# Linear attention, a routed expert layer and a feed-forward layer in one kernel: batchwise attention in four chain groups, filler on the first weights, rows gathered seven tiles ahead

## The chip, the cores and the metric

The kernel runs on one core of a Trainium2 chip. A core has a matrix engine (PE, with its weight loads shown apart as PEld), three engines for elementwise work (DVE, ACT, POOL), a queue processor that issues transfers (SP) and 16 DMA engines. The metric is the device time of one execution in microseconds (us), less is better; several runs are taken and their median counts. A profile is one more execution with its trace.

## The reference, cut to what matters

```python
kv  = einsum('bhsd,bhse->bhde', k, v)           # 4 batches, 8 heads, 576 rows, 64 wide
out = einsum('bhsd,bhde->bhse', q, kv)
x   = out / sqrt(mean(out**2) + 1e-6) * g_norm  # as 2304 rows of 512
logits = x @ w_gate                             # 8 experts
e, gate = argmax(logits), softmax(logits)[argmax]
# rows in order of arrival go to their expert, at most `capacity` (576) each
h = relu(rows_e @ w1[e]); y = h @ w2[e]         # 512 -> 1024 -> 512 per expert
x2[row] = gate * y
h2 = x2 @ w_in; g = where(h2 > 0, h2, exp(h2) - 1)
result = g @ w_out                              # 512 -> 2048 -> 512
```

## The kernel before, in words

All products are in float32; the large ones are done as three products of split operands (a rounded high part and the remainder; `three`, L585). There are 18 tiles of 128 rows.

**Attention** (L57 to L360). SP issues the loads of k and v chunk by chunk (`load_kv`) and of q in pieces (`load_q`), then the stores of the results to `x_dram`, in one queue. The order of everything else is written out by hand between `fill(6)` and the last `step(cc, ...)`. `kv_product(b, n0, n1)` multiplies chunks of a batch, `kv_out`, `kv_turn` and `kv_gate` turn the product into the matrix `kva[b]`, which has eight gate columns per head beside the values, `out_tile(i)` multiplies the rows of tile i by it, and ACT and POOL copy and square the result. `out_sums(i)` adds the squares on DVE. `fill(n)` issues n products of a constant on PE that nothing reads; `fill(n, t)` first waits for the tile t.

**Chains and dispatch** (L223 to L452). `chain(i0, G)` computes the norm, the gate logits and the one-hot choice `oh` of G tiles together, 17 small steps that `step(c, n)` advances, most of them on DVE. The groups hold 4, 5 and 9 tiles. When the last group has its `oh`, two products count the rows per expert (`p_tot`, `p_pos`), a scan (`incl`) and some twenty DVE instructions make the permutation, and `p_inv` gives `ids`, the row numbers in expert order.

**Experts** (L505 to L860). POOL gathers the permuted rows from `x_dram` tile by tile (`gather`, L491) into buffers `xg`, of which there are three; DVE scales a tile (`place_scale`, L497), PE transposes it (`place_turn`, L503) and ACT copies it to `xT`. The gather of tile a+3 stands behind the transposes of tile a, which free its buffer. The experts come in order of their row count, in windows of 352, 336, ... rows. A unit u is one of the 8 chunks of one expert's hidden width: `expert_h(u)` is 12 products into a PSUM tile `ph`, `expert_y(u)` 12 products into `acc`. `step(u)` loads the weights of unit u+3, runs `expert_h(u)`, places a row tile or more, runs `expert_y(u-1)`, places more, and splits the weights of unit u+2 (on ACT, DVE and POOL). `QUOTA` gives how many tiles the units of the first expert place; before unit 6 all 18 have to be placed, 3 in `first_window` and 15 in the units 0 to 5.

**Feed-forward** (L820 to L925). 96 steps in which PE multiplies for 4.2 us each; the loads and splits of these weights are spread over all units.

Of the kernel before, what the change touches and what calls it, by code (L numbers as in the profile page):

```python
# [9 lines left out]
F32 = mybir.dt.float32  # L10
# [31 lines left out]
def block_kernel(ctx, tc, qT, k, v, g_norm, w_gate, w1, w2, w_in, w_out, out, cap, **_):  # L42
# [62 lines left out]
    with ExitStack() as actx:  # L105
# [80 lines left out]
        groups = [(0, 4), (4, 5), (9, 9)]  # L186
        GM = 9
# [35 lines left out]
        def chain(i0, G):  # L223

            def t_(shape, name):
                full = ap2.tile([P, GM] + shape, F32, name=name)
                return full[:, :G]
# [53 lines left out]
        for c in range(9, 18):  # L281
            load_kv(c)
        load_q(2, [(0, 256), (256, S)])
        load_q(3, [(0, 192), (192, 448), (448, S)])
        fill(6)

        ca, cb, cc = (chain(*g) for g in groups)
        for c in range(5):
            kv_product(0, c, c + 1)
            fill(3 if c < 4 else 0)  # L290
        kv_out(0)
        kv_product(1, 0, 1)
        fill(1)
# [5 lines left out]
        kv_product(1, 1, 3)  # L299
        out_tile(1)  # L300
        out_sums(0)
        out_tile(2)
        out_sums(1)
        kv_product(1, 3, 5)
        kv_out(1)
        out_tile(3)
        out_sums(2)
        kv_turn(1)
        fill(3)
        kv_gate(1)  # L310
        out_sums(3)
        fill(1)
        step(ca, 2)
        out_tile(4)
        step(ca, 4)
        kv_product(2, 0, 2)
        out_tile(5)
        out_sums(4)
        step(ca, 4)
        kv_product(2, 2, 4)  # L320
        out_tile(6)
        out_sums(5)
        step(ca, 3)
        kv_product(2, 4, 5)
        kv_out(2)
        kv_product(3, 0, 1)
        fill(2)
        kv_turn(2)
        out_sums(6)
        step(ca, 4)  # L330
        out_tile(7)
        kv_gate(2)
        out_sums(7)
        kv_product(3, 1, 3)
        out_tile(8)
        out_sums(8)
        step(cb, 2)
# [3 lines left out]
        fill(2)  # L341
        kv_turn(3)
        step(cb, 2)
        fill(2)
        kv_gate(3)
        fill(1)
        step(cb, 1)
        for i in range(9, NT):
            out_tile(i)
            if i > 9:  # L350
                out_sums(i - 1)
            step(cb, 2 if i < 14 else 1 if i == 14 else 0)
        out_sums(17)
        fill(6)
        step(cc, 2)
        fill(3, flat(made[9]["a"]))
        step(cc, 2)
        fill(2, flat(made[9]["e"]))
        step(cc, 2)
        fill(2, flat(made[9]["z"])[:, 0:P])  # L360
        step(cc, 2)
        fill(1, flat(made[9]["lg"]))
        step(cc, 4)
# [11 lines left out]
        step(cc, 5)  # L375
# [11 lines left out]
        nc.vector.tensor_tensor(out=pos, in0=incl, in1=p_pos, op=ALU.add)  # L387
        before = t_(EE, "before")
        nc.vector.tensor_tensor(out=before, in0=key[:, None, :].to_broadcast(EE), in1=key.to_broadcast(EE), op=ALU.is_gt)
        off, kept = vals[:, 1], vals[:, 2]  # L390
# [3 lines left out]
        fill(4, flat(bk))  # L394
# [12 lines left out]
        nc.vector.tensor_reduce(out=tab, in_=rr, axis=AX, op=ALU.add)  # L407
        dest = t_([P, NT], "dest")
        nc.vector.tensor_reduce(out=dest, in_=pos.rearrange("p e c -> p c e"), axis=AX, op=ALU.add)
        nc.vector.tensor_copy(tabi, tab[0:1])  # L410
        fill(4, flat(tab))
# [8 lines left out]
        fill(2, flat(oa))  # L420
# [70 lines left out]
    def gather(a):  # L491
# [464 lines left out]
```

## Time and profile before

| | us |
|---|---|
| median of three runs | 724.04 (721.87 to 725.79) |
| the profiled execution | 721.96 |
| its span | 720.2 |
| PE busy in the span | 692.4 (96%) |
| DVE, ACT, POOL busy | 425.3, 347.8, 96.9 |
| mean granted clock of PE | 0.982 |

Times in the trace run from the span's start. The share of PE is an average: in the long stretch of experts and feed-forward it is without a gap, and the gaps are all in the first 126 us. The granted clock is 1.00 at PE's upper level (2.4 GHz) and 0.50 at its lower one (1.2 GHz).

### The profile page before, as it was taken

What the parts mean: (1) busy time and instruction counts of PE and PEld (TensorE: products, weight loads), DVE (VectorE), ACT (ScalarE), POOL (GpSimd) and SP (SyncE); (2) the same over time, 40 slices, a digit from 0 to 9 for tenths busy, and PEclk for the clock granted to TensorE, in tenths of its full rate; (3) what the DMA queues carried; (4) which work ended last, traced back from release to release, by engine and by line L of the source; (5) the groups of instructions that cost most, each with busy time, mean ns of one, the idle gap of its engine ahead of it and who ended that gap; (6) DMA issues with size and microseconds to landing.
All of it is one profiled execution on the core that took longest, in us unless ns stands there. A gap on an engine that the chain in (4) does not pass through costs nothing.

```text
span 720.2 us, 11582 instructions
## 1 busy us (share of the span) xinstructions
PE 692.4 (96%) x4310; PEld 645.6 (90%) x4310; DVE 425.3 (59%) x789; ACT 347.8 (48%) x689; POOL 96.9 (13%) x108
## 2 busy tenths in 40 slices
PE   7997787999999999999999999999999999999996
PEld 6987787999998999999999998998999999899895
DVE  4567655767876878655555545666994334333342
ACT  1552554455555655566566554444654334333331
POOL 7121472000000000052222000000000000011122
PEclk9998798999999999999999999999999999999999
DMA  8995774556555657435335434333542223233312
GB/s 286 397 304 142 218 214 130 176 172 197 170 181 155 218 165 253 133 132 190 146 118 217 163 117 147 118 146 118 196 154 90 103 115 119 101 132 131 132 45 87
DMA packets 55423, 117.53 MB, mean 163 GB/s; under 512 B 8000, under 2 KB 21824, under 8 KB 55360
## 3 DMA queue, kind: packets, MB, share of 16 engines
q1 hardware_dynamic: 51744, 107.12, 43.8%
q0 software_dynamic: 2880, 9.59, 3.9%
q8 instruction: 36, 0.59, 0.3%
q14 instruction: 27, 0.22, 0.1%
q10 hardware_dynamic: 736, 0.02, 0.1%
HBM read 97.68 MB, written 19.02 MB: 162 GB/s over the span
## 4 chain that ended last, share of the span: by engine, by line
PE 59%; issue 8%; POOL 1%; POOLq 0%; DVE 0%
PE ph L587 10%; PE ph L589 10%; PE ph L588 10%; PE acc L887 8%; PE acc L888 8%; PE acc L886 8%; PE acc L589 2%; PE acc L587 2%; PE acc L588 2%; POOL out L897 1%; POOLq L952 0%; DVE part L894 0%; POOLq L897 0%
## 5 line engine op out<-in xcount | busy, mean ns | idle before, releaser
L867 DVE SCALAR_TENSOR_TENSOR g<-e,ph 128x384 f32<-128x384 f32 x96 | 53.0, 552 | 133.6 <-ACT e L865 133.3
L589 PE MATMUL ph<-yl,w1h 128*128 128x384 f32 x384 | 129.5, 337 | 0.0
L587 PE MATMUL ph<-yh,w1h 128*128 128x384 f32 x384 | 129.3, 337 | 0.0
L588 PE MATMUL ph<-yh,w1l 128*128 128x384 f32 x384 | 129.0, 336 | 0.0
L864 ACT ACTIVATE e<-ph 128x384 f32<-128x384 f32 x96 | 47.2, 492 | 160.8 <-PE ph L589 160.7
L888 PE MATMUL acc<-w2h,gl 128*128 128x512 f32 x288 | 114.0, 396 | 0.0
L887 PE MATMUL acc<-w2l,gh 128*128 128x512 f32 x288 | 113.7, 395 | 0.0
L886 PE MATMUL acc<-w2h,gh 128*128 128x512 f32 x288 | 112.0, 389 | 0.0
L587 PE MATMUL ph<-xh,w1h 128*128 128x288 f32 (+6 forms) x256 | 79.2, 309 | 2.4 <-PEq L734 1.7
L589 PE MATMUL ph<-xl,w1h 128*128 128x288 f32 (+6 forms) x256 | 78.5, 306 | 0.0
L588 PE MATMUL ph<-xh,w1l 128*128 128x288 f32 (+6 forms) x256 | 78.4, 306 | 0.0
L587 PE MATMUL acc<-hh,w2h 128*128 128x288 f32 (+6 forms) x256 | 77.5, 303 | 0.0
L588 PE MATMUL acc<-hh,w2l 128*128 128x288 f32 (+6 forms) x256 | 77.0, 301 | 0.0
L589 PE MATMUL acc<-hl,w2h 128*128 128x288 f32 (+6 forms) x256 | 76.9, 301 | 0.0
L587 PEld LDWEIGHTS ph<-yh,w1h 128*128 128x128 f32 x384 | 72.2, 188 | 4.2
L588 PEld LDWEIGHTS ph<-yh,w1l 128*128 128x128 f32 x384 | 72.1, 188 | 4.1
L589 PEld LDWEIGHTS ph<-yl,w1h 128*128 128x128 f32 x384 | 72.0, 188 | 0.0
L480 ACT ACTIVATE gh<-g 128x384 fp32r<-128x384 f32 x96 | 50.4, 525 | 43.1 <-DVE g L867 41.3
L483 DVE TENSOR_TENSOR gl<-g,gh 128x384 fp32r<-128x384 f32 x96 | 55.7, 580 | 18.1 <-ACT gh L480 18.1
L606 ACT ACTIVATE hh<-ph 128x288 fp32r<-128x288 f32 (+6 forms) x64 | 27.1, 423 | 81.0 <-PE ph L589 81.0
L888 PEld LDWEIGHTS acc<-w2h,gl 128*128 128x128 f32 x288 | 54.0, 187 | 11.6
L887 PEld LDWEIGHTS acc<-w2l,gh 128*128 128x128 f32 x288 | 54.0, 187 | 9.2
(157 smaller groups left out, 1188.1 us busy)
## 6 DMA issues: line engine op xcount, KB each, us to landing
a<-w SPq DMA_DIRECT2D x128, 256.0 KB
yh<-y_dram SPq DMA_DIRECT2D x18, 768.0 KB
yl<-y_dram SPq DMA_DIRECT2D x18, 768.0 KB
w<-w_in SPq DMA_DIRECT2D x16, 512.0 KB
w<-w_out SPq DMA_DIRECT2D x16, 512.0 KB
kt<-k SPq DMA_DIRECT2D x18, 256.0 KB
vt<-v SPq DMA_DIRECT2D x18, 256.0 KB
x_dram<-oz_all SPq DMA_DIRECT2D x18, 256.0 KB
```

The source lines that it names most:

```text
L480: return nc.scalar.activation(dst[0], src, AF.Copy)
L483: return engine.tensor_tensor(out=dst[1], in0=src, in1=dst[0].bitcast(F32), op=ALU.subtract)
L587: nc.tensor.matmul(out, lhsT=ah, rhs=bh, start=start, stop=False)
L588: nc.tensor.matmul(out, lhsT=al, rhs=bh, start=False, stop=False)
L589: nc.tensor.matmul(out, lhsT=ah, rhs=bl, start=False, stop=stop)
L606: nc.scalar.activation(hh[:, :W], ph[:, :W], AF.Relu)
L864: nc.scalar.activation(e, ph[:, :BT], AF.Relu, scale=-1.0)
L867: nc.vector.scalar_tensor_tensor(out=g, in0=e, scalar=-1.0, in1=ph[:, :BT], op0=ALU.add, op1=ALU.max)
L886: nc.tensor.matmul(acc, lhsT=gh[:, ts], rhs=w2h, start=(c == 0), stop=False)
L887: nc.tensor.matmul(acc, lhsT=gh[:, ts], rhs=w2l, start=False, stop=False)
L888: nc.tensor.matmul(acc, lhsT=gl[:, ts], rhs=w2h, start=False, stop=(c == NC2 - 1))
L897: put = nc.gpsimd.indirect_dma_start(out=out, out_offset=bass.IndirectOffsetOnAxis(ap=ids[:, i:i + 1], axis=0), in_=part[:, i], in_offset= ...
```

## The change

Five edits that are made together.

1. Attention in another hand-written order: q of batch 2 is loaded before the last four chunks of k and v, out tiles 9 to 12 stand between the steps of batch 3, and most fillers of this part are gone. In the first five chunks a filler now reads the chunk of k that has landed.
2. Four chain groups of 4, 5, 3 and 6 tiles. The addition of 1e-9 to the softmax's sum and the product `rr` move from DVE to POOL, and the conversion `tabi` stands before `dest` on DVE.
3. In the dispatch the fillers behind `oa` are fewer, and one more group waits for `incl`.
4. 16 products of a constant with the first four weight tiles, in the order of their landing, behind the 14 fillers that follow `p_inv`.
5. Four more row buffers (`lent`), lent by the second pair of window buffers, so that seven gathers stand at the front; the gather of tile a+7 stands behind the transposes of tile a. Two PSUM tiles for the transposed rows and two for `ph`, in place of one and three. `QUOTA` is 2 for the units 0 to 5. The weights of unit 2 wait for the third gather, not the second. The staging pool of the weights is allocated first, over the space of k and v.

```diff
-        groups = [(0, 4), (4, 5), (9, 9)]
+        groups = [(0, 4), (4, 5), (9, 3), (12, 6)]
...
-            yield V.tensor_scalar(out=sm, in0=sm, scalar1=1e-9, scalar2=None, op0=ALU.add)
-            yield V.reciprocal(out=sm, in_=sm)
-            V.tensor_tensor(out=rr, in0=r[:, :, None, :].to_broadcast([P, G, 2, H]), in1=sm.to_broadcast([P, G, 2, H]), op=ALU.mult)
+            yield nc.gpsimd.tensor_scalar(out=sm, in0=sm, scalar1=1e-9, scalar2=None, op0=ALU.add)
+            V.reciprocal(out=sm, in_=sm)
+            nc.gpsimd.tensor_tensor(out=rr, in0=r[:, :, None, :].to_broadcast([P, G, 2, H]), in1=sm.to_broadcast([P, G, 2, H]), op=ALU.mult)
...
-        for c in range(9, 18):
+        for c in range(9, 14):
             load_kv(c)
         load_q(2, [(0, 256), (256, S)])
+        for c in range(14, 18):
+            load_kv(c)
         load_q(3, [(0, 192), (192, 448), (448, S)])
...
         kv_out(3)
         step(cb, 1)
-        fill(2)
+        out_tile(10)
         kv_turn(3)
+        out_sums(9)
+        step(cb, 3)
+        out_tile(11)
+        kv_gate(3)
...
-        fill(2, flat(oa))
+        fill(2, flat(tab))
+        fill(0, flat(oa))
...
+    wst = ctx.enter_context(tc.tile_pool(name="wst", bufs=2, reuse_waits="tile"))
     xw = ctx.enter_context(tc.tile_pool(name="xw", bufs=2, reuse_waits="tile"))
     hp = ctx.enter_context(tc.tile_pool(name="hp", bufs=3, reuse_waits="tile"))
-    wst = ctx.enter_context(tc.tile_pool(name="wst", bufs=2, reuse_waits="tile"))
...
-    ps_h = ctx.enter_context(tc.tile_pool(name="ps_h", bufs=3, space=PSUM, reuse_waits="tile"))
-    ps_x = ctx.enter_context(tc.tile_pool(name="ps_x", bufs=1, space=PSUM, reuse_waits="tile"))
+    ps_h = ctx.enter_context(tc.tile_pool(name="ps_h", bufs=2, space=PSUM, reuse_waits="tile"))
+    ps_x = ctx.enter_context(tc.tile_pool(name="ps_x", bufs=2, space=PSUM, reuse_waits="tile"))
...
-    XG = 3
+    XG, XE = 3, 4
...
+    def gather():
+        a = gathered["n"]
+        if a >= NT:
+            return
+        gathered["n"] += 1
+        k = a % (XG + XE)
+        if k >= XG:
+            xg_t[a] = lent[k - XG]
+        else:
+            xg_t[a] = wst.tile([P, C + 2 * H], F32, name="xg", tag="w64", bufs=XG)
...
-    QUOTA = (1, 2, 2, 3, 2, 2, 3, 0)
+    QUOTA = (2, 2, 2, 2, 2, 2, 3, 0)
...
-        gathers = [gather(a) for a in range(XG)]
+        for tag in ("xh", "xl"):
+            t = xw.tile([P, XE // 2, C + 2 * H], F32, name="lent", tag=tag)
+            lent.extend(t[:, n] for n in range(XE // 2))
+        gathers = [gather() for _ in range(XG + XE)]
+
+        idle = ps_h.tile([P, C], F32, name="idle", tag="ph")
+        for t in wstage[0] + wstage[1]:
+            for _ in range(4):
+                nc.tensor.matmul(idle[:, 0:P], lhsT=ident, rhs=t[:, 0:P], start=True, stop=True)
         expert_split(0, nc.vector)
         expert_split(1, nc.vector)
         first_window()
-        tc.add_manual_dep(expert_load(2).ins, gathers[1].ins.name, ...)
+        tc.add_manual_dep(expert_load(2).ins, gathers[2].ins.name, ...)
```

POOL at the beginning of the experts, before: `L494 DMA` rows are gathers, `w1l` is POOL's share of a weight split, one per unit.

```order
L383 COPY vals<-row 128x8
L494 DMA xg<-x_dram,ids 128x528 x7
L483 TENSOR_TENSOR w1l<-a_1022,w1h 128x512
L494 DMA xg<-x_dram,ids 128x528 x2
L483 TENSOR_TENSOR w1l<-a_1028,w1h 128x512
L494 DMA xg<-x_dram,ids 128x528 x2
L483 TENSOR_TENSOR w1l<-a_1066,w1h 128x512
L494 DMA xg<-x_dram,ids 128x528 x3
```

POOL at the same place after the change (L542 gathers, L521 splits):

```order
L419 COPY vals<-row 128x8
L256 TENSOR_TENSOR rr<-r,sm 128x96
L542 DMA xg<-x_dram,ids 128x528 x3
L542 DMA lent<-x_dram,ids 128x528 x4
L542 DMA xg<-x_dram,ids 128x528 x3
L542 DMA lent<-x_dram,ids 128x528 x2
L521 TENSOR_TENSOR w1l<-a_1078,w1h 128x512
L542 DMA lent<-x_dram,ids 128x528 x2
L521 TENSOR_TENSOR w1l<-a_1084,w1h 128x512
L542 DMA xg<-x_dram,ids 128x528 x2
L521 TENSOR_TENSOR w1l<-a_1129,w1h 128x512
```

Seven gathers wait for no row buffer, where three did; 12 of the 18 stand before the first split in place of 7.

PE from `p_inv` to the first products of unit 0, before (`pt` are transposes of rows, four to a tile; `ob` is a weight of `p_inv`):

```order
L437 LDWEIGHTS ob
L437 MATMUL p_inv<-oat,ob 128x18
L120 MATMUL idle<-ident 128x128 x14
L561 MATMUL pt<-ident,xg 128x128 x12
L587 MATMUL ph<-xh,w1h 128x352
L588 MATMUL ph<-xh,w1l 128x352
L589 MATMUL ph<-xl,w1h 128x352
```

PE at the same place after the change:

```order
L475 LDWEIGHTS ob
L475 MATMUL p_inv<-oat,ob 128x18
L120 MATMUL idle<-ident 128x128 x14
L884 MATMUL idle<-a_990,ident 128x128 x4
L884 MATMUL idle<-a_991,ident 128x128 x4
L884 MATMUL idle<-a_994,ident 128x128 x4
L884 MATMUL idle<-a_995,ident 128x128 x4
L609 MATMUL pt<-ident,xg 128x128 x12
L635 MATMUL ph<-xh,w1h 128x352
```

The transposes of the first window stand behind 16 products that wait for the four weight tiles.

DVE from the last `oh` to the scan, before (`sm` is the softmax's sum, `incl` the scan's result):

```order
L250 TENSOR_TENSOR oh<-sel,m_767 128x9x8
L253 TENSOR_REDUCE sm<-ex 128x9
L254 TENSOR_SCALAR sm<-sm 128x9
L255 RECIPROCAL sm<-sm 128x9
L256 TENSOR_TENSOR rr<-r,sm 128x144
L377 SCALAR_TENSOR_TENSOR incl<-reset,p_tot 128x144
```

DVE at the same place after the change:

```order
L250 TENSOR_TENSOR oh<-sel,m_791 128x6x8
L255 RECIPROCAL sm<-sm 128x5
L255 RECIPROCAL sm<-sm 128x3
L253 TENSOR_REDUCE sm<-ex 128x6
L413 SCALAR_TENSOR_TENSOR incl<-reset,p_tot 128x144
```

The last `oh` is of 6 tiles, not 9; three instructions stand between it and the scan where four stood, two of them left over from the groups before, and the last group's own reciprocal has moved behind the scan.

## Rows read from the trace of the kernel before

**Rows 1.** Stretches (us): each engine's busy time (instructions), granted clock, DMA share, GB/s.

```profile
53.75:67.70 13.95, 11.25 (x77) 9.95 (x78) 11.49 (x41) 3.09 (x9) 0.00 (x0) 0.76 0.51 107
67.70:78.10 10.40, 5.83 (x40) 5.20 (x38) 7.50 (x17) 4.43 (x8) 5.02 (x5) 0.76 0.81 247
78.10:126.30 48.20, 41.53 (x240) 39.45 (x241) 25.07 (x34) 25.25 (x44) 24.86 (x23) 0.88 0.60 180
126.30:700.00 573.70, 571.97 (x3308) 535.92 (x3307) 343.25 (x619) 289.29 (x578) 39.31 (x37) 1.00 0.42 149
```

**Rows 2.** The same view, cut where the granted clock changes.

```profile
73.00:83.30 10.30, 7.52 (x29) 6.50 (x29) 5.82 (x9) 4.31 (x8) 2.93 (x3) 0.50 0.80 267
114.00:120.80 6.80, 6.00 (x22) 5.62 (x23) 2.76 (x3) 3.31 (x6) 1.28 (x1) 0.50 0.02 5
```

**Rows 3.** PE's waits from 78 to 126.4: us in total, times, longest.

```profile
PE pt L507 <- DVE xg L500: 4.3, 3, 2.5
```

**Rows 4.** DVE's waits in the same stretch.

```profile
DVE xg L500 <- DMA xg<-x_dram,ids: 13.7, 7, 3.1
```

**Rows 5.** Timeline of PE (start, duration): the first products of five units.

```profile
78.11 0.66 PE L587 MATMUL ph<-xh,w1h 128*128 128x352 f32 x1 [0.67 <-ACT xh L563]
...
88.00 0.40 PE L587 MATMUL ph<-xh,w1h 128*128 128x352 f32 x1
...
92.71 0.40 PE L587 MATMUL ph<-xh,w1h 128*128 128x352 f32 x1
...
122.48 0.32 PE L587 MATMUL ph<-xh,w1h 128*128 128x352 f32 x1
...
126.31 0.32 PE L587 MATMUL ph<-xh,w1h 128*128 128x336 f32 x1
```

**Rows 6.** Timeline of the first and third gather, and of the third tile's scaling.

```profile
68.71 1.17 POOL L494 DMA_INDIRECT xg<-x_dram,ids  x1 [16.79 <-DMA a<-w]
...
71.59 0.95 POOL L494 DMA_INDIRECT xg<-x_dram,ids  x1 [0.30 <-issue]
...
75.45 0.75 DVE L500 SCALAR_TENSOR_TENSOR xg<-xg,used 128x512 f32<-128x512 f32 x1 [0.24 <-DMA xg<-x_dram,ids]
```

**Rows 7.** Stretch of attention, PE's fillers alone: PE and PEld busy, clock, DMA, GB/s.

```profile
17.30:52.00 34.70, 3.80 (x22) 2.92 (x22) 1.00 1.11 355
```

**Rows 8.** Timeline of DVE: the last group's chain and the scan.

```profile
53.79 0.20 DVE L234 TENSOR_SCALAR a<-sums 128x72 f32<-128x72 f32 x1
...
55.42 0.76 DVE L241 TENSOR_TENSOR z<-oz_all,r 128x576 f32<-128x576 f32 x1
56.21 1.19 DVE L244 TENSOR_REDUCE lg<-z 128x72 f32<-128x576 f32 x1
...
58.50 0.47 DVE L250 TENSOR_TENSOR oh<-sel,m 128x72 f16<-128x72 f32 x1
...
59.82 0.46 DVE L377 TENSOR_TENSOR_SCAN incl<-reset,p_tot 128x144 f32<-128x144 f32 x1
```

**Rows 9.** Groups by line and shape: z and lg of five tiles (busy us, mean ns).

```profile
L244 DVE TENSOR_REDUCE lg<-z 128x40 f32<-128x320 f32 x1 | 0.7, 728 | 0.0
...
L241 DVE TENSOR_TENSOR z<-oz_all,r 128x320 f32<-128x320 f32 x1 | 0.5, 492 | 0.0
```

**Rows 10.** Timeline of the end of the dispatch.

```profile
64.06 1.95 DVE L433 TENSOR_TENSOR ob<-neg,nb 128x768 f16<-128x768 f16 x2
...
66.91 0.60 PE L437 MATMUL p_inv<-oat,ob 128*128 128x18 f16 x18
...
67.55 0.18 DVE L445 TENSOR_SCALAR ids<-p_inv 128x18 uint32<-128x18 f32 x1 [1.24 <-PE p_inv L437]
```

**Rows 11.** Timeline of one hand-over of `ph`: last product, DVE's read, next-but-one product.

```profile
292.03 0.28 PE L589 MATMUL ph<-xl,w1h 128*128 128x256 f32 x1
...
292.76 0.42 DVE L607 SCALAR_TENSOR_TENSOR hl<-ph,hh 128x256 fp32r<-128x256 f32 x1
...
296.45 0.28 PE L587 MATMUL ph<-xh,w1h 128*128 128x256 f32 x1
```

More of the change, by code (lines that the diff above doesn't have):

```diff
@@ L225, in t_ @@
             def t_(shape, name):
-                full = ap2.tile([P, GM] + shape, F32, name=name)
+                full = ap2.tile([P, GM] + shape, F32, name=name, bufs=3)
                 return full[:, :G]
@@ L280, in block_kernel, with chunk @@
         load_q(1, [(0, 320), (320, S)])
-        for c in range(9, 18):
+        for c in range(9, 14):
             load_kv(c)
         load_q(2, [(0, 256), (256, S)])
+        for c in range(14, 18):
+            load_kv(c)
         load_q(3, [(0, 192), (192, 448), (448, S)])
+        def chunk(b, n, after):
+            fill(1, kt[(b // 2) * 9 + (b % 2) * 4 + n][:, 0:P])
+            kv_product(b, n, n + 1)
+            fill(after)
+        ca, cb, cc, cd = (chain(*g) for g in groups)
         fill(6)
-        ca, cb, cc = (chain(*g) for g in groups)
         for c in range(5):
-            kv_product(0, c, c + 1)
-            fill(3 if c < 4 else 0)
+            chunk(0, c, (3, 3, 4, 3, 0)[c])
         kv_out(0)
         kv_product(1, 0, 1)
-        fill(1)
         kv_turn(0)
@@ L340, in block_kernel @@
         step(cb, 1)
-        fill(2)
+        out_tile(10)
         kv_turn(3)
-        step(cb, 2)
-        fill(2)
-        kv_gate(3)
-        fill(1)
-        step(cb, 1)
[L348 to L352, printed above, removed]
+        out_sums(9)
+        step(cb, 3)
+        out_tile(11)
+        kv_gate(3)
+        out_sums(10)
+        step(cb, 2)
+        out_tile(12)
+        out_sums(11)
+        step(cb, 3)
+        step(cc, 1)
+        out_tile(13)
+        step(cc, 1)
+        out_sums(12)
+        step(cb, 2)
+        step(cc, 2)
+        out_tile(14)
+        step(cb, 1)
+        out_sums(13)
+        step(cc, 2)
+        out_tile(15)
+        out_sums(14)
+        step(cc, 3)
+        out_tile(16)
+        out_sums(15)
+        step(cc, 1)
+        out_tile(17)
+        step(cc, 2)
+        out_sums(16)
         out_sums(17)
+        L = groups[-1][0]
         fill(6)
[L355 to L363, printed above, removed]
+        step(cd, 1)
+        step(cb, 1)
+        step(cd, 1)
+        step(cc, 1)
+        fill(3, flat(made[L]["a"]))
+        step(cc, 1)
+        step(cd, 2)
+        fill(2, flat(made[L]["e"]))
+        step(cd, 2)
+        fill(2, flat(made[L]["z"])[:, 0:P])
+        step(cb, 1)
+        step(cc, 1)
+        step(cd, 2)
+        fill(1, flat(made[L]["lg"]))
+        step(cd, 4)
+        step(cb, 1)
+        step(cc, 1)
         def t_(shape, name, dt=F32):
@@ L374, in block_kernel @@
         fill(2)
-        step(cc, 5)
+        step(cd, 3)
         incl = t_([P, E, NT], "incl")
@@ L486, in ring_tiles @@
         return [ring.tile([P, C], F32R, name=n) for n in ("w1h", "w1l", "w2h", "w2l")]
-    XG = 3
+    XG, XE = 3, 4
     xg_t = {}
-    def gather(a):
-        if a < NT:
+    lent = []
+    gathered = {"n": 0}
+    def gather():
[7 more added lines that the diff above has]
+        else:
             xg_t[a] = wst.tile([P, C + 2 * H], F32, name="xg", tag="w64", bufs=XG)
-            return nc.gpsimd.indirect_dma_start(out=xg_t[a], out_offset=None, in_=x_dram,
-                                         in_offset=bass.IndirectOffsetOnAxis(ap=ids[:, a:a + 1], axis=0))
+        return nc.gpsimd.indirect_dma_start(out=xg_t[a], out_offset=None, in_=x_dram,
+                                            in_offset=bass.IndirectOffsetOnAxis(ap=ids[:, a:a + 1], axis=0))
     def place_scale(a):
@@ L508, in place_turn @@
         nc.scalar.activation(xT[:, :, a * P:(a + 1) * P], pt, AF.Copy, scale=g_col)
-        gather(a + XG)
+        gather()
     offs, eids = {}, {}
@@ L563, in first_window @@
             nc.scalar.activation(xh[:, :, w], pt[:, :, :w.stop - w.start], AF.Copy, scale=g_col)
-            gather(a + XG)
+            gather()
             pts.append(pt)
```

53 lines of the change are left out of this document (29 added, 24 removed).

## The prediction

> **What bounds the kernel now.** I read the stretches first. From 126.3 us to 700 PE is busy 571.97 of 573.70 us at the upper clock [rows 1]: nothing that the change does ahead of 126.3 can hide there, and what is won or lost before moves the end by as much. The change touches only what lies before, so the question is when the second expert starts (126.31, the last of [rows 5]). Three stretches lead to it. Attention up to 52 us is bound by the loads: 355 GB/s and a DMA share above 1, with PE at the upper clock and 22 filler instructions in it [rows 7]. From 53.75 to 67.7 the chain of the last group and the permutation run on DVE (11.49 of 13.95 us busy). From 67.7 to 78.1 the rows and the first weights arrive and PE is busy for 5.83 of 10.40 us. From 78.1 to 126.3 the first expert runs: the clock is 0.88 in the mean and the DMA share only 0.60 [rows 1].
>
> The waits tell why. In the first expert PE waits 4.3 us for scaled rows [rows 3], and DVE, before it can scale them, 13.7 us in seven waits for gathers [rows 4]. The gather of tile a+3 starts only when tile a is transposed; the first gather starts at 68.71 and the third at 71.59, yet the third tile is scaled at 75.45 [rows 6]: some 4 us from issue to use. With three buffers the row supply is a loop of that latency. The idle time has a second price: the clock stood at 0.50 from 73.0 to 83.3 and from 114.0 to 120.8, each time after PE had idled [rows 2].
>
> **The change part by part.**
>
> *Attention and dispatch, up to `ids` (67.73 in the trace, from [rows 10]: 67.55 + 0.18).* PE loses 14 of its 22 filler instructions here (11 fills become 4); at 2.92/22 = 0.133 us each that is 1.8 us of PE [rows 7]. But DVE now has the chain of three more tiles to do before the last sums, some 2.7 us (z and lg at about 0.16 and 0.23 us less than those of [rows 9] for two tiles fewer, eleven more instructions at 0.2 like the first of [rows 8]), late, since the data arrive late. I give PE 1.8 and take most of it back on DVE: the last sums end 0.5 us earlier (bounds: 1.8 earlier, 0.9 later, when DVE takes all of its 2.7). Then the last chain: with 6 tiles between the rows of 5 and 9, z takes 0.492 + (0.757 - 0.492)/4 = 0.56 in place of 0.76 us and lg 0.84 in place of 1.19, and seven small instructions some 0.02 less each [rows 8, 9]: 0.7 us. Between `oh` (ends at 58.97) and the scan (59.82) three instructions of 0.2 stand for 0.85 us, which wins 0.25; the reciprocal that now comes behind the scan costs 0.2: nothing. POOL's two new instructions per group feed only the store of `rr` and that reciprocal, with some 1 us of DVE work before it; if POOL were late there, DVE would stand still for as long. Last, `p_inv` starts at 66.91 although `ob` is ready at 64.06 + 1.95 = 66.01 [rows 10]: PE was held by fillers at the lower clock. With four fewer of their instructions behind `oa` 0.7 of these 0.9 us go. Sum: `ids` 1.9 us earlier (bounds: 3.4 earlier, 0.9 later).
>
> *From `ids` to the first product of unit 0: 78.11 - 67.73 = 10.38 us.* What ends last is the third tile. POOL's distance from gather to gather stays, so its scaling ends at `ids` + 8.47 (75.45 + 0.75 - 67.73) [rows 6]. From there 1.9 us were transposes and copies at the lower clock. The 16 new products read weights that land before the rows, so at the upper clock (32 instructions of 0.133 us, 4.3 us, from the end of the 14 fillers at about `ids` + 3) they end at about `ids` + 7.3, ahead of the third tile; PE goes into the transposes without the idle time of before: 0.6 us (bounds: 1 us, or a loss of 2, when they run at the lower clock and the transposes stand behind them). The weights no longer wait for the end of `ob`, which takes them off the DMA engines when the rows come; I count that as nothing.
>
> *The first expert: 48.2 us.* When nothing waits, a unit with two tiles takes 92.71 - 88.00 = 4.71 us and one without 126.31 - 122.48 = 3.83 [rows 5]. With seven gathers ahead, tile a+7 is requested three units before its use, some 14 us, against the 4 us of latency. So: unit 0 has no `expert_y` (4.71 - 1.92 = 2.8), units 1 to 4 take 4 x 4.71 = 18.84, unit 5 has three tiles more, at DVE's 0.75 each [rows 6] since two PSUM tiles now let PE run ahead of ACT's copies (4.71 + 2.25 = 6.96), units 6 and 7 take 2 x 3.83 = 7.66. Sum 36.3 us: 11.9 less (bounds: 13 less, when unit 5's tiles cost PE alone; nothing, when the rows come no faster). POOL has two gathers of 1.3 and a split of 1.3 us in a unit of 4.71, so it keeps up. The same bytes, 180 GB/s x 48.2 us = 8.7 MB, in 36.3 us are 239 GB/s; the core moved 247 with the same mixture just before [rows 1] and 267 at its densest [rows 2]. That is close, and is the second rival.
>
> *Two PSUM tiles for `ph`, for all 160 units and steps.* The read-out of a `ph` ends at 292.76 + 0.42 = 293.18, and the next-but-one product starts at 296.45 [rows 11]: 3.3 us to spare where the products are shortest. Cost: nothing.
>
> Sum: 1.9 + 0.6 + 11.9 = 14.4 us off the span of 720.2; with the 1.76 us around it the profiled execution's 721.96 become 707.6. It lies 2.1 below the median of its runs. Part of their scatter of 3.9 us must be where in the clock's changes the waits fall, and most of those waits go; I take half of the 2.1 and forecast 708.5.
>
> **Rivals.** *A cold start.* PE still waits between the last filler and unit 0, with 12 transposes in some 3 us. In the trace such a stretch ended at 1.2 GHz: from 73.0 to 83.3 [rows 2]. Then unit 0's product takes twice its 1.92 us and the transposes 0.3 more, about +2.2, and if it lasts as long as before (10.3 us at half speed) 5 us: 710.7 to 713.5, taken as 711. For it: the wait for the third tile stays. Against: the filler ends some 1 us before that tile, not 3. The Trainium skill's page "TensorE: Matmul & The Clock Gate" (Part 1) says that "the default state is throttled, and activity releases the throttle"; by that rule fillers protect the clock only while they run, and this rival is what it makes of the change. The trace agrees with it, at 0.50 after both idle stretches.
>
> *The transfers set the pace.* If the DMA engines give no more than the middle of 180 and 247 GB/s, 213, the first expert's 8.7 MB take 40.8 us and 7.4 are won there: 713. For it: in this stretch the engines are already 0.60 busy, and gathers and weights share them. Against: DVE waited for a gather that had been issued late, not for one in a queue.
>
> *Only attention and dispatch give something,* and the rows stay as late (a lent buffer comes free too late, say): 2.5 us, 719.5 to 721.5, no change.
>
> *Slower: two `ph` are too few.* If the read-out of `ph` came over 3.3 us later than now, PE would wait in each unit and step. The gain is lost from 0.09 us in each of 160; at 0.2 us, net 18 us later: 726. For it: DVE is the busiest of the engines behind PE, and it reads each `ph`. Against: PE never waited for it in 573.7 us, and the spare time is 3.3 us.
>
> **How the numbers follow.** Forecast 0.57, cold start 0.24, transfers 0.12, no change 0.04, slower 0.03. About 0.5% (3.6 us) is what a measurement can tell from no change: faster takes the first three, 0.93, same 0.04, slower 0.03. The likeliest case has 704.5 (all terms at their good ends but the 0.9 of DVE) to 710.5; the range reaches through the cold start and half of the transfers' case: 704.5 to 713.
>
> **What would show it.** Seven gathers on POOL at distances of 1.3 us right behind `ids`; `ids` at 65.8; unit 0 at about 75.6 with the granted clock at 1.00; units 1 to 4 each 4.7 us apart; PE's wait for scaled rows under 1 us; the second expert at about 111.9 in place of 126.31, and the rest as long as before, 594 us. Wrong it is if DVE's waits for gathers stay near 13.7 us, if the DMA share from unit 0 on is above 0.9 with PE waiting, or if PE waits for DVE's `hl` or `g`.

## The result, and the profile after

The changed kernel takes 711.79 us (median of four runs, 710.62 to 712.05) against 723.35 (721.87 to 725.79) for the kernel before on the same chip: 0.9829 of it, 95% interval 0.9803 to 0.9855. The forecast was 708.5 in a range of 704.5 to 713: faster, as forecast, by 11.6 us in place of some 15. A second series of the changed kernel gave 711.29 (ratio 0.9836, 0.9815 to 0.9857).

The profiled execution took 710.62 us, with a span of 708.7. The page has PE busy for 689.5 us (97%) at a mean granted clock of 0.998. Its stretches, cut at the same four events as [rows 1] (length; busy time and instructions of PE, PEld, DVE, ACT, POOL; granted clock; DMA share; GB/s):

```profile
54.89:66.74 11.85, 9.27 (x73) 7.32 (x74) 10.38 (x42) 3.46 (x11) 1.78 (x7) 1.00 0.57 140
66.74:75.85 9.11, 8.11 (x71) 7.64 (x70) 7.25 (x16) 4.10 (x8) 6.97 (x7) 1.00 0.72 193
75.85:112.90 37.05, 36.32 (x240) 35.09 (x241) 27.66 (x35) 24.91 (x44) 24.33 (x21) 1.00 0.70 232
112.90:688.90 576.00, 572.61 (x3310) 536.37 (x3309) 343.38 (x620) 289.81 (x579) 39.12 (x37) 1.00 0.43 149
```

The first expert has shrunk from 48.20 to 37.05 us, PE is busy for 36.32 of them, and the clock is 1.00 where it was 0.88. The same rows and weights now come at 232 GB/s with the DMA share at 0.70, so the transfers did not set the pace over the whole of it. The last row has a loss: PE is idle for 3.4 us there, against 1.7 in [rows 1].

PE's waits in the first expert (us in total, times, longest), which answer to [rows 3]:

```profile
PE ph L635 <- ACT xh L611: 0.7, 1, 0.7
PE pt L555 <- ACT xT L556: 0.3, 1, 0.3
PE pt L555 <- PE pt L555: 0.3, 1, 0.3
```

No wait for scaled rows is left (4.3 us before). DVE's waits for gathers, the 13.7 us of [rows 4], are now:

```profile
DVE lent L548 <- DMA lent<-x_dram,ids: 3.0, 3, 1.2
```

These 3.0 us are early, while POOL issues gather after gather: the fifth, sixth and seventh gather are issued at 72.67, 74.08 and 75.60 and DVE can scale their rows from 78.28, 80.66 and 82.12, 5.6 to 6.6 us later and not 4. PE feels 0.3 of these waits: the last of its three lines above is the second tile of unit 0, whose row is scaled only at 79.03. The gathers on POOL stand right behind `ids` (66.74), 1.25 to 1.63 us apart (start, duration):

```profile
67.04 1.33 POOL L542 DMA_INDIRECT xg<-x_dram,ids  x1 [5.78 <-DMA a<-w]
68.67 1.18 POOL L542 DMA_INDIRECT xg<-x_dram,ids  x1 [0.30 <-issue]
70.16 0.95 POOL L542 DMA_INDIRECT xg<-x_dram,ids  x1 [0.30 <-issue]
71.41 0.96 POOL L542 DMA_INDIRECT lent<-x_dram,ids  x1 [0.30 <-issue]
```

PE's timeline from `p_inv` to the second expert, cut to the fillers, the transposes of the first three tiles and the first products of the units 0, 1, 2 and of the second expert (112.91, 126.31 in [rows 5]):

```profile
66.38 3.37 PE L120 MATMUL idle<-ident 128*128 128x128 f32 x28
69.58 3.74 PE L884 MATMUL idle<-a,ident 128*128 128x128 f32 x32
73.16 1.04 PE L609 MATMUL pt<-ident,xg 128*128 128x128 f32 x8
74.52 0.66 PE L609 MATMUL pt<-ident,xg 128*128 128x128 f32 x4 [0.33 <-DVE xg L548]
75.85 0.43 PE L635 MATMUL ph<-xh,w1h 128*128 128x352 f32 x1 [0.67 <-ACT xh L611]
...
79.52 0.41 PE L635 MATMUL ph<-xh,w1h 128*128 128x352 f32 x1
...
84.31 0.41 PE L635 MATMUL ph<-xh,w1h 128*128 128x352 f32 x1
...
112.91 0.32 PE L635 MATMUL ph<-xh,w1h 128*128 128x336 f32 x1
```

Up to the second expert 13.4 us are gone. The span is shorter by 11.5 only, so 1.9 came back later, in a stretch of which the forecast said that nothing changes. PE's waits behind the second expert's start show where. Before:

```profile
PE ph L587 <- PEq L734: 1.7, 1, 1.7
```

After:

```profile
PE ph L635 <- ACTq L782: 2.4, 1, 2.4
PE acc L636 <- issue: 1.0, 1, 1.0
```

L734 and L782 are the same statement: the conditional pass over rows beyond the windows (`beyond_windows`), which this input never enters. All engines test a value there and jump over the pass, and PE has nothing to do until its own jump is done.

### The profile page after: what moved, and what is told of

It reads as the page before. It is cut to its first block, busy times and chain, and to the rows that moved or that the text cites. A ratio compares the mean times of both kernels' runs of the same rounds, so it can differ in the third digit from the quotient of the medians.

```text
span 708.7 us, 11682 instructions
## 1 busy us (share of the span) xinstructions
PE 689.5 (97%) x4344; PEld 643.1 (91%) x4344; DVE 428.9 (61%) x796; ACT 347.8 (49%) x692; POOL 100.4 (14%) x116
## 4 chain that ended last, share of the span: by engine, by line
issue 45%; PE 22%; POOL 2%; POOLq 0%; ACT 0%
PE ph L635 4%; PE ph L637 4%; PE ph L636 4%; PE acc L636 2%; PE acc L635 2%; PE acc L637 2%; POOL out L953 2%; PE acc L943 1%; PE acc L944 1%; PE acc L942 1%; POOL yl L521 1%; POOLq L1008 0%; ACT yh L518 0%; ACT e L920 0%; POOLq L953 0%
## 5 line engine op out<-in xcount | busy, mean ns | idle before, releaser
L521 DVE TENSOR_TENSOR gl<-g,gh 128x384 fp32r<-128x384 f32 x96 | 54.9, 571 | 19.0 <-ACT gh L518 19.0
L944 PEld LDWEIGHTS acc<-w2h,gl 128*128 128x128 f32 x288 | 54.0, 188 | 11.6
```

Of the source, the lines that this page charges most:

```text
L521: return engine.tensor_tensor(out=dst[1], in0=src, in1=dst[0].bitcast(F32), op=ALU.subtract)
L944: nc.tensor.matmul(acc, lhsT=gl[:, ts], rhs=w2h, start=False, stop=(c == NC2 - 1))
```

## The experiments

Each kernel was timed against the kernel before, in four to twelve runs. Medians and ratios are of those runs; the other columns are from each kernel's profiled execution: the end of `ids`, from there to the first product of unit 0, from there to the second expert, and the rest of the span (us).

| kernel | median | ratio to before (95%) | `ids` | to unit 0 | first expert | rest |
|---|---|---|---|---|---|---|
| before | 723.35 | 1 | 67.73 | 10.38 | 48.20 | 593.9 |
| changed | 711.79 | 0.9829 (0.9803-0.9855) | 66.74 | 9.11 | 37.06 | 595.8 |
| changed, again | 711.29 | 0.9836 (0.9815-0.9857) | 66.44 | 10.18 | 36.72 | 596.1 |
| rows only | 713.05 | 0.9855 (0.9833-0.9878) | 68.27 | 9.98 | 38.47 | 596.0 |
| three buffers | 722.24 | 0.9981 (0.9964-0.9997) | 66.11 | 9.29 | 48.67 | 596.4 |
| five buffers | 711.75 | 0.9844 (0.9823-0.9866) | 67.58 | 10.47 | 37.04 | 595.7 |
| no filler | 711.30 | 0.9836 (0.9817-0.9855) | 66.47 | 9.34 | 38.06 | 594.7 |
| fillers between | 711.63 | 0.9827 (0.9811-0.9844) | 66.23 | 9.28 | 37.97 | 594.7 |
| PSUM 3 and 1 | 719.16 | 0.9932 (0.9910-0.9953) | 67.03 | 12.55 | 41.34 | 595.5 |
| the same, no filler | 715.98 | 0.9890 (0.9871-0.9909) | 67.02 | 9.71 | 41.54 | 595.8 |
| spread QUOTA | 716.09 | 0.9885 (0.9862-0.9909) | 66.40 | 12.55 | 39.35 | 598.6 |
| three groups | 712.76 | 0.9845 (0.9820-0.9869) | 65.75 | 9.92 | 38.06 | 595.9 |
| three groups, fillers between | 709.47 | 0.9801 (0.9788-0.9815) | 65.12 | 10.04 | 37.52 | 594.6 |
| no branch | 709.55 | 0.9816 (0.9788-0.9844) | 66.72 | 11.39 | 37.80 | 591.9 |

### How much is the rows' part, and what in it

**Rows only**: the kernel before with edit 5 and nothing else.

```diff
-    XG = 3
+    XG, XE = 3, 4
...
-    QUOTA = (1, 2, 2, 3, 2, 2, 3, 0)
+    QUOTA = (2, 2, 2, 2, 2, 2, 3, 0)
...
-    ps_h = ctx.enter_context(tc.tile_pool(name="ps_h", bufs=3, space=PSUM, reuse_waits="tile"))
-    ps_x = ctx.enter_context(tc.tile_pool(name="ps_x", bufs=1, space=PSUM, reuse_waits="tile"))
+    ps_h = ctx.enter_context(tc.tile_pool(name="ps_h", bufs=2, space=PSUM, reuse_waits="tile"))
+    ps_x = ctx.enter_context(tc.tile_pool(name="ps_x", bufs=2, space=PSUM, reuse_waits="tile"))
```

> The kernel before with edit 5 alone (seven gathers ahead, two and two PSUM tiles, QUOTA, the weights of unit 2 behind the third gather). My theory: attention and dispatch stay (ids at 67.7), the first expert falls from 48.2 us to about 37 as in the changed kernel, but unit 0 starts at the lower clock, since PE idles before it as it did before: 2.2 to 5 us of that come back. Second expert at 117 to 120, time 713 to 716 against 723.4 before. Rival (rows alone are the whole gain, the other edits nothing): 711 to 712. Rival (rows count only together with the filler's clock): 718 or more.

713.05 us: edit 5 alone has 10.2 of the gain, and the other four together some 1.3, which is not clear of the scatter (the two intervals overlap). Unit 0 did start at the lower clock (0.55 from 76.3 to 83.9 us), as the theory said, and the first expert took 38.47 us in place of 37.06.

**Three buffers** and **five buffers**: the changed kernel with no lent row buffer, and with two.

```diff
-    XG, XE = 3, 4
+    XG, XE = 3, 0
...
-        for tag in ("xh", "xl"):
-            t = xw.tile([P, XE // 2, C + 2 * H], F32, name="lent", tag=tag)
-            lent.extend(t[:, n] for n in range(XE // 2))
```

> The changed kernel with no lent row buffers (three in all, the gather of tile a+3 behind the transposes of tile a), all else as changed. My theory: the row supply is again a loop of some 4 us for three tiles; DVE's waits for gathers in the first expert come back from 3.0 us to 10 or more, the second expert starts 8 to 11 us later, time 719 to 723. Rival (the first expert became shorter by the warm clock and the second pair of PSUM tiles, not by the number of buffers): 712 to 714.

```diff
-    XG, XE = 3, 4
+    XG, XE = 3, 2
```

> The changed kernel with two lent row buffers in place of four: five gathers ahead. My theory: a loop of 4 us for five tiles supplies one each 0.8 us, units need one each 2.35; nothing lost but POOL's order: 711 to 713, second expert at 113 to 114. Rival (every buffer counts, in proportion between three and seven): 715 to 717.

With three the whole gain is gone (722.24), though everything else is as changed; with five nothing is lost (711.75). In the profile with three buffers DVE's and PE's waits of the first expert are back, and larger than before the change:

```profile
DVE xg L548 <- DMA xg<-x_dram,ids: 20.0, 10, 3.6
```

```profile
PE pt L555 <- DVE xg L548: 7.5, 5, 2.5
```

The first expert takes 48.67, 37.04 and 37.06 us with three, five and seven buffers. Two of the four lent buffers buy nothing. But a loop of 4 us that is too slow is not what the three buffers show: it would give a row each 1.3 us, and a unit with two tiles wants one each 2.35. The first products of the units 0, 2, 3, 4 and 5 with three buffers:

```profile
75.40 0.43 PE L635 MATMUL ph<-xh,w1h 128*128 128x352 f32 x1 [0.67 <-ACT xh L611]
...
88.49 0.41 PE L635 MATMUL ph<-xh,w1h 128*128 128x352 f32 x1
...
93.21 0.41 PE L635 MATMUL ph<-xh,w1h 128*128 128x352 f32 x1
...
97.92 0.41 PE L635 MATMUL ph<-xh,w1h 128*128 128x352 f32 x1
...
102.90 0.40 PE L635 MATMUL ph<-xh,w1h 128*128 128x352 f32 x1
```

The units 2 and 3, with two tiles each, take 4.72 and 4.71 us, as in the changed kernel: there three buffers keep up. The time goes in unit 0 (7.40 us against 3.66), where the fourth gather is issued at 73.40, behind the transposes of the first tile, and its row is scaled only from 79.58; and in unit 5 (11.13 against 6.73), which wants five tiles at once. The granted clock adds to it, with 0.50 from 81.5 to 84.9 us and 0.51 from 112.2 to 119.1. So the buffers that pay are a stock for the start and for the five tiles of unit 5; four buffers were not tried.

**PSUM 3 and 1**: the changed kernel with three tiles for `ph` and one for the transposed rows.

```diff
-    ps_h = ctx.enter_context(tc.tile_pool(name="ps_h", bufs=2, space=PSUM, reuse_waits="tile"))
-    ps_x = ctx.enter_context(tc.tile_pool(name="ps_x", bufs=2, space=PSUM, reuse_waits="tile"))
+    ps_h = ctx.enter_context(tc.tile_pool(name="ps_h", bufs=3, space=PSUM, reuse_waits="tile"))
+    ps_x = ctx.enter_context(tc.tile_pool(name="ps_x", bufs=1, space=PSUM, reuse_waits="tile"))
```

> The changed kernel with three PSUM tiles for ph and one for the transposed rows, as before. My theory: the pair of ph tiles costs nothing, so the units behind the first expert stay 50.24 us for 12 steps; each tile placed right behind another waits for ACT's copy, so unit 0 (3.66) grows by 0.3 to 0.6 us and unit 5 (6.73) by 1 to 2: 713 to 714.5. Rival (one PSUM tile for the rows is enough): 711 to 712. Rival (two ph tiles cost something in each step): faster than the changed kernel, 708 to 710.

719.16, against an expected 713 to 714.5. Unit 5 took 9.01 us against 6.73, as the theory says, but unit 0 came 12.55 us behind `ids`. To see whether that belongs to the PSUM tiles, the same without the products on the first weights:

```diff
-        idle = ps_h.tile([P, C], F32, name="idle", tag="ph")
-        for t in wstage[0] + wstage[1]:
-            for _ in range(4):
-                nc.tensor.matmul(idle[:, 0:P], lhsT=ident, rhs=t[:, 0:P], start=True, stop=True)
```

> The changed kernel with three PSUM tiles for ph and one for the transposed rows, and without the 16 products on the first weights. My theory: of the 7.4 us that the one PSUM tile for rows seemed to cost, only the growth of unit 5 (9.01 against 6.73) and some 0.5 of unit 0 are its own; 3.4 us (unit 0 at 12.55 behind ids) and the lower clock after it belong to the products on the weights that stand ahead of the transposes. Without them unit 0 comes at 9.3 to 10 behind ids, unit 5 stays at 9.0: 713.5 to 715. Rival (one PSUM tile makes the first window late, products or not): 717 to 720.

715.98, one us above my theory's range and one below the rival's, with unit 0 at 9.71 behind `ids` and unit 5 at 9.01 us long again. Against the kernel without filler and with two tiles (711.30) the medians differ by 4.7 us; they are of two series, and by the ratios to the kernel before it is 3.9. The profiles have the same 3.9 from `ids` to the second expert (51.25 against 47.40 us), most of it in unit 5 (9.01 against 6.72) and unit 0 (5.88 against 4.40); what the spans differ by beyond that lies before `ids` and at the jump. So one PSUM tile costs some 3.9 us. PE's timeline of unit 5 in this kernel shows how:

```profile
107.20 0.66 PE L555 MATMUL pt<-ident,xg 128*128 128x128 f32 x4 [0.78 <-ACT xT L556]
108.64 0.65 PE L555 MATMUL pt<-ident,xg 128*128 128x128 f32 x4 [0.78 <-ACT xT L556]
110.07 0.66 PE L555 MATMUL pt<-ident,lent 128*128 128x128 f32 x4 [0.78 <-ACT xT L556]
```

A tile behind another starts 1.44 us after it: 0.66 for the transposes and 0.78 of waiting for ACT's copy out of the only PSUM tile. In the changed kernel the last two stand 0.59 apart:

```profile
104.17 0.66 PE L555 MATMUL pt<-ident,xg 128*128 128x128 f32 x4 [0.34 <-ACT xT L556]
104.76 0.66 PE L555 MATMUL pt<-ident,lent 128*128 128x128 f32 x4
```

Two `ph` tiles in place of three cost nothing: twelve units from the second expert's second one on take 43.39 us in every one of the fourteen profiles, with two or with three.

**Spread QUOTA**: unit 5's extra tiles moved to units 1 to 3.

```diff
-    QUOTA = (2, 2, 2, 2, 2, 2, 3, 0)
+    QUOTA = (2, 3, 3, 3, 2, 2, 3, 0)
```

> The changed kernel with QUOTA 2, 3, 3, 3, 2, 2 for the units 0 to 5 in place of 2 in each: the three tiles left over in unit 5 are placed in units 1 to 3. My theory: PE takes 0.44 us for a tile (4.71 less 3.83 for two), so unit 5 falls from 6.73 to about 4.7 and units 1 to 3 grow by 0.44 to 0.75 each: nothing to 0.7 us less, 711 to 712. Rival (the rows are not there so early, seven gathers ahead are not enough for three tiles a unit): DVE waits for gathers again, units 2 and 3 over 6 us, 713 to 715.

Slower than the changed kernel, 716.09, and neither theory had it. The gathered rows were there (DVE has no wait for a gather in these units); but a unit with three tiles took 5.71 us, 1.0 more than one with two, so that three of them cost 3.0 and unit 5 gave back 2.0. My 0.44 us a tile, half the difference between two tiles and none, does not hold for a third. Each third tile makes PE stand still for some 0.4 us:

```profile
89.31 0.63 PE L555 MATMUL pt<-ident,xg 128*128 128x128 f32 x4 [0.39 <-issue]
```

The profile names no releaser, but DVE scales this tile from 88.47 to 89.21 us, just before: `place_ahead(2)` has only two tiles scaled ahead. The profile with spread QUOTA is of its slowest run (718.81), so that its other losses, unit 0 at 12.55 us behind `ids` and a jump that cost more than elsewhere (rest 598.6), need not all be in the median.

### The products on the first weights

**No filler** (the four lines above that make `idle` and its products, taken out of the changed kernel):

> The changed kernel without the 16 products on the first weights. My theory: PE idles 3 to 4 us between the 14 fillers and the first tile, the granted clock falls to 0.50 before unit 0 and stays there for some units: 2 to 5 us longer, 714 to 717, second expert at 115 to 118. Rival (the clock recovers at once since the rows no longer let PE wait, or doesn't fall): within 1 us, 711 to 713.

711.30, the same as with them, where I expected 714 to 717. The clock did fall, to 0.50 from 75.8 to 79.2 us, and units 0 and 1 together were 9.45 us long in place of 8.46, 0.74 of that in unit 0; but unit 0 came 9.34 us behind `ids`, as early as with them. What the fillers win at the clock they can lose by standing ahead of the transposes. In the changed kernel's second profile the granted clock was at 0.50 from 65.5 to 68.9 us, the 14 fillers behind `p_inv` took 4.70 us in place of 3.37, and the 16 products behind them ended at 74.36, 2.8 us after the first tile had been scaled and 0.05 after the third:

```profile
66.08 4.70 PE L120 MATMUL idle<-ident 128*128 128x128 f32 x28
70.62 3.74 PE L884 MATMUL idle<-a,ident 128*128 128x128 f32 x32
74.19 1.47 PE L609 MATMUL pt<-ident,xg 128*128 128x128 f32 x12
76.62 0.43 PE L635 MATMUL ph<-xh,w1h 128*128 128x352 f32 x1 [0.95 <-ACT xh L611]
```

All twelve transposes then stand in one piece behind the fillers, and unit 0 starts at 10.18. Of the eight profiles with the 16 products four show this: two have unit 0 at 10.18 and 10.47 us behind `ids`, two at 12.55, where something else is added (see the last section). In the other four the products end in time, 6.6 us behind `ids`; there unit 0 starts at 9.11 and 9.29 or, with the other delay, at 9.92 and 11.39.

**Fillers between**: one product for each weight tile, and fillers in the gaps between the tiles.

```diff
-            for _ in range(4):
+            for _ in range(1):
                 nc.tensor.matmul(idle[:, 0:P], lhsT=ident, rhs=t[:, 0:P], start=True, stop=True)
...
             for j in range(NP):
                 nc.tensor.transpose(pt[:, j], xg[:, j * P:(j + 1) * P], ident)
+            for _ in range(3 if a + 1 < need[0] else 2):
+                nc.tensor.matmul(idle[:, 0:P], lhsT=ident, rhs=ident, start=True, stop=True)
```

> The changed kernel with one product on each of the four first weight tiles in place of four, and fillers between the transposes of the first three tiles instead (3 behind the first, 3 behind the second, 2 behind the third). My theory: the 16 products end 6.6 us behind ids at the upper clock and 8.2 at the lower one, where they push the transposes (first tile scaled at 4.8) and unit 0 back; spread over the gaps they keep PE busy without standing ahead of a tile. Unit 0 at 9.0 to 9.4 us behind ids, no lower clock in units 0 and 1: 710 to 711.3. Rival (the clock falls anyway, or PE's place in front of unit 0 doesn't matter): 711.3 to 712.5.

Unit 0 came at 9.28 at the full clock, as expected, but the time is 711.63, in the rival's range and within the scatter of the changed kernel. What unit 0 won (3.15 us in place of 3.66) the units 1 and 2 lost (5.17 and 5.65 in place of 4.79 and 4.72), where PE waited 0.3 us for ACT and 0.7 us for POOL's share of a weight split. No gain of the clock and of the place of these fillers can be told from the scatter here.

### The four chain groups

**Three groups**: the new order of attention with the groups of before. `cc` becomes an empty iterator, so that its steps do nothing.

```diff
-        groups = [(0, 4), (4, 5), (9, 3), (12, 6)]
-        GM = 6
+        groups = [(0, 4), (4, 5), (9, 9)]
+        GM = 9
...
-                full = ap2.tile([P, GM] + shape, F32, name=name, bufs=3)
+                full = ap2.tile([P, GM] + shape, F32, name=name)
...
-        ca, cb, cc, cd = (chain(*g) for g in groups)
+        ca, cb, cd = (chain(*g) for g in groups)
+        cc = iter(range(99))
```

> The changed kernel with the chain groups of before (4, 5, 9 tiles) in the new order of attention. My theory: the extra chain of three tiles keeps DVE busy ahead of the last sums, so that these end 2.31 us after PE's last out tile (1.41 before the change); without it that distance falls to 1.4 to 1.7 us, the last chain grows from 4.5 to 5.2 us; the two cancel, ids within 0.5 us of 66.1 to 67.6, time 711 to 712.5. Rival (the shorter last chain of the four groups is a net gain): ids 0.7 us later or more, distance as in the changed kernel, 712.5 to 713.5.

The time is 712.76, no better, and in the rival's range; but the rival's sign, an `ids` that comes 0.7 us later, is not there. The profile bears my mechanism out: DVE's last sums end 1.48 us behind PE's last out tile, against 2.30 or 2.31 in all ten profiles with four groups and 1.40 in the two with the attention of before. DVE in the changed kernel (three tiles' chain among the sums, which end at 54.89):

```profile
52.50 0.68 DVE L213 TENSOR_REDUCE sums<-sq 128x8 f32<-128x512 f32 x1
53.09 0.17 DVE L248 SCALAR_TENSOR_TENSOR sel<-sh,rev_e 128x24 f32<-128x24 f32 x1
53.30 0.18 DVE L249 TENSOR_REDUCE m<-sel 128x3 f32<-128x24 f32 x1
53.52 0.26 DVE L250 TENSOR_TENSOR oh<-sel,m 128x24 f16<-128x24 f32 x1
53.62 1.27 DVE L213 TENSOR_REDUCE sums<-sq 128x8 f32<-128x512 f32 x2
54.92 0.19 DVE L234 TENSOR_SCALAR a<-sums 128x48 f32<-128x48 f32 x1
```

With three groups the last five tiles' sums run in one piece and end at 53.20:

```profile
50.08 3.12 DVE L213 TENSOR_REDUCE sums<-sq 128x8 f32<-128x512 f32 x5
53.23 0.20 DVE L234 TENSOR_SCALAR a<-sums 128x72 f32<-128x72 f32 x1
```

So the sums end 0.83 us sooner behind the out tile, and the last chain takes 5.21 us in place of 4.52: of the two only 0.14 us is left. `ids` came at 65.75 and 65.12 us in the two profiles with three groups, at 66.11 to 67.58 in the ten with four; the rest of that lies before the chains, since PE's last out tile ended at 51.72 and 51.06 there and at 51.96 to 53.26 in the ten, and why is open. **Three groups with the fillers between** puts the two together:

> The same with the three chain groups of before (4, 5, 9). My theory: ids came at 65.75 us in the profile with three groups against 66.1 to 67.6 (seven profiles) with four, and the gain was hidden by a late unit 0 (9.92 us behind ids): 709.3 to 711. Rival (ids with three groups is no earlier, one profile is scatter): as the kernel with the fillers between alone, or up to 1 us more.

709.47 us (709.13 to 710.40), 0.9801 of before. To have a measure for it, the changed kernel was run again:

> The changed kernel itself once more, as the measure for the kernel with three groups and the fillers between (709.47, 0.9801 of before, 0.9788 to 0.9815). My theory (three groups bring ids about 1.2 us earlier, the fillers between keep unit 0 from coming late): 711 to 712.5, ratio 0.983 to 0.985, last sums behind 54 us, unit 0 between 9.1 and 10.5 us behind ids. Rival (709.47 is the scatter between series): ratio at or under 0.981.

711.29 (710.66 to 712.88), ratio 0.9836, 0.9815 to 0.9857. That interval begins where the other's ends; the one of the first series (from 0.9803) overlaps it. All nine runs of the changed kernel lie above the five of this version, so it is probably faster than the changed kernel too, by some 2 us; the two were not timed side by side. In the profiles 1.2 to 1.5 us of the difference lie behind the second expert's start (594.6 against 595.8 and 596.1), at the jump of the next section, which neither groups nor fillers are meant to touch. Whether the groups have any part in the 2 us stays open, since three groups alone gave 712.76 and the fillers alone 711.63.

### The jump

**No branch**: the changed kernel without the conditional pass.

```diff
             place(NT, 0)
-            beyond_windows()
```

> The changed kernel without the conditional pass over rows beyond the windows (this input has none, so that the skipped code is never run; the kernel leaves out only the test, the jump and the code behind it). My theory: behind the second expert's start everything but the place of that jump repeats to 0.1 us from kernel to kernel; at the jump PE stands still for 1.7 us before the change and 3.4 us after it, which is what made the rest 1.9 us longer than forecast. Without it 3 to 4 us less: 707.5 to 709. Rival (the stall is only shown there, and PE would wait for weights or splits instead): 711 to 712.

From the second expert's start to the end 591.9 us pass in place of 595.8, and PE has no wait at all there. So the jump costs 3.9 us in the changed kernel's profile and 2.0 in that of before. Over the thirteen profiles with it the cost runs from 2.0 to 6.7 us (spread QUOTA). It is not all waiting: in six of the thirteen the granted clock stands at 0.50 soon behind the jump. With five buffers, for one, PE stands still for 2.0 us, the clock is at 0.50 from 218.1 to 221.5 us, and the jump costs 3.8. The time without it is 709.55, half a microsecond above my range, in a kernel whose profile has unit 0 late again (11.39); its six runs lie between 709.24 and 713.77.

## Why the prediction was right, and where it was off

**What bounds the kernel.** Right: the second expert's start moved by 13.4 us and the end followed, but for the jump.

**The first expert.** Forecast 36.3 us, measured 37.06. Units 1 to 4 took 18.93 (18.84 forecast), unit 5 6.73 (6.96), units 6 and 7 7.74 (7.66). The miss is unit 0: 3.66 in place of 2.8, since I took a unit of 4.71 less its `expert_y`. Its products took 2.36 in place of 1.92 us (75.85 to 78.21, at the start still behind DVE's `xl`), and without `expert_y` between them its two tiles' transposes stand close, where the second waits for its row. That too few buffers were the cause is shown by three and five buffers. The prediction's reason, a supply that is a loop of 4 us, is right in part: PE did wait for rows that were asked for too late, but as a rate the loop would have been fast enough, and with three buffers the loss was at the start and in unit 5. And it is not the rows alone: with one PSUM tile some 3.9 us of the gain are lost. The prediction had that in unit 5's term, as a price of 0.75 a tile, and nowhere said what it costs if the second tile is missing.

**From `ids` to unit 0.** Forecast 0.6 less, measured 1.27 less in this profile and 0.20 in the second one (10.18). The 16 products took 3.74 us where I had 4.3: my 0.133 us an instruction came from PEld's column of [rows 7], and back to back one takes 0.117. The bound "a loss of 2, when they run at the lower clock and the transposes stand behind them" has its mechanism in half of the profiles with these products, but not its size: where nothing else is added unit 0 starts 1.07 and 1.36 us later than in the first profile.

**`ids` 1.9 us earlier: the step that failed in size.** It came 0.99 earlier. The last chain (0.69 shorter), the scan (0.54 sooner behind `oh`) and `p_inv` (scan to `ids` 0.89 shorter) are as forecast or better; of the last, though, some 0.8 is there in rows only too, whose dispatch is that of before, so that it is not shown to come from the fewer fillers. Wrong is "the last sums end 0.5 us earlier": they ended 1.13 later, beyond the 0.9 that I gave as the worst. I gave PE 1.8 us for the fillers taken out, but PE's last out tile ended at 52.58 against 52.36, no earlier; the DVE term of some 2.7 us then stood alone, and 0.9 of it appears as 2.31 less 1.40 us between out tile and sums. One pair of profiles can't say more of the out tile: with the attention of before it ended at 52.36 and 53.68, with the new one at 51.06 to 53.26.

**The rest as long as before, 594 us.** Wrong by 1.9 us. The edits do not touch the jump, and I counted on PE never waiting there, though the row of before shows 571.97 busy in 573.70 us: the 1.7 us between them were this jump, so that the long stretch was not without a gap before either, and I did not ask what set its length.

**The sum.** 0.99 + 1.27 + 11.14 - 1.89 = 11.5 us off the span (720.2 to 708.7), 14.4 forecast. The median lies 1.17 above the profiled execution in place of the 0.9 that I added. The likeliest case ended at 710.5; that the range holds 711.79 is owed to what was added for other cases, which did not happen, and to that extent it is luck.

**The rivals.** 711 was the time of the cold start, and the measured time is near it, but not by its mechanism: the granted clock was 1.00 from 40 to 140 us in the profile. The Trainium skill's rule ("TensorE: Matmul & The Clock Gate", Part 1, activity releases the throttle) agrees with the kernel without filler, where the clock fell; its price was 1.0 us there at most, not 2.2 to 5. Transfers at 213 GB/s did not decide: 232 were reached. Two `ph` tiles were not too few; the sum of that rival was wrong besides, since 0.2 us in each of 160, 32 us, less the gain of 14.4 would have made some 742, not 726.

## What to carry to other kernels

Where buffers are refilled behind their last use, latency divided by their number says only whether they keep up at an even pace; here three did in the units 2 and 3. Count them for the start and for the largest burst as well (five did what seven did, with bursts of five), and look at what frees the next stage's buffer too, since a second PSUM tile was worth some 3.9 us here. Splitting a late chain into more groups shortens its last link, but the fixed cost of the extra group falls on the engine that the last link waits for. Fillers that stand in a queue ahead of real work delay it when they happen to run at the lower clock. And a stretch that a change does not touch need not keep its length: the jump alone moved by 1.9 us.

## What the hardware showed that I had not expected

**A two-input operation of DVE stood still for POOL's.** In the new order `z` of five tiles takes 1.29 us, against 0.492 in [rows 9], in every one of the profiles with it. DVE and POOL in the changed kernel:

```profile
44.95 1.29 DVE L241 TENSOR_TENSOR z<-oz_all,r 128x320 f32<-128x320 f32 x1
...
47.74 0.70 DVE L246 TENSOR_TENSOR sh<-lg,mx 128x40 f32<-128x40 f32 x1
```

```profile
44.86 1.04 POOL L206 TENSOR_TENSOR sq<-oz_all 128x512 f32<-128x512 f32 x1 [3.46 <-issue]
47.34 1.04 POOL L206 TENSOR_TENSOR sq<-oz_all 128x512 f32<-128x512 f32 x1 [1.44 <-ACT oz_all L205]
```

Both of DVE's started while one of POOL's ran, 0.09 and 0.40 us after its start, and ended 0.34 and 0.06 us after it; `sh`, 0.19 us for five tiles before the change, took 0.70. The next `z`, of three tiles, starts 0.31 us ahead of a square of POOL's and takes 0.36, in line with 0.49 for five. The two delays are 1.3 us of DVE in the stretch where DVE sets the pace. The Trainium skill has the rule ("SBUF — State Buffer", Who interferes with whom): an operation of DVE with two inputs in SBUF and one of POOL that reads SBUF share a port as an exclusive lock, and the later one blocks. The trace agrees on who is held up, and roughly on how long: a `sh` that had stood still to the very end of POOL's could not end 0.06 us after it. Moving POOL's squares by a microsecond was not tried.

**A jump over code that is never run holds PE for microseconds, and not for the same time in each kernel.** The jump itself takes PE's sequencer (PEldq below) 3.34 us before the change and 3.9 after it (0.05 to 0.07 us on SP, ACT and DVE), and PE runs out of products meanwhile:

```profile
L734 PEldq COMPARE_BRANCH  x1: 3340/3340/3340, 224.9 to 224.9; - x1
```

```profile
L782 PEldq COMPARE_BRANCH  x1: 3905/3905/3905, 211.5 to 211.5; - x1
```

Five transfers of the kind "instruction" run between 211.4 and 215.9 us of the changed kernel's profile, so that fetching the code behind the jump is the likely cause; that was not tested.

**Unit 0 can be late by more than the records of PE explain.** With spread QUOTA the twelve transposes are recorded from 74.45 to 75.92 us, but ACT, which by the trace waits for these alone, reads the first at 77.16:

```profile
77.16 1.74 ACT L611 ACTIVATE xh<-pt,g_col 128x512 fp32r<-128x512 f32 x3 [7.59 <-PE pt L609]
```

PSUM 3 and 1 shows the same (2.3 us), no branch and three groups a part of it; all of them have the 16 products, and no kernel without them shows it. In all four the granted clock stands at 0.50 soon after (from 80.1 us with spread QUOTA), as it did behind idle time in [rows 2], so that PE was probably idle as its records say. In three of them, not in no branch, a transfer of the kind "instruction" ends 0.1 to 0.3 us before ACT's first reading. What ACT waited for stays open.
